# Sigmoid attention and a gated feed-forward layer on one core: another order of the step table

## The chip, the cores and the metric

The kernel runs on one core of one Trainium2 chip. The metric is the device time of one execution in microseconds. The engines are named as in the profile: PE (TensorE, matmuls), DVE (VectorE), ACT (ScalarE), POOL (GpSimd) and SP (SyncE). POOL and SP also issue the transfers: loads go through POOL's queue, stores through SP's.

## The reference

Two layers follow each other. The first is attention with a sigmoid in place of the softmax, over 8 batches, 12 heads, 448 tokens and a head size of 64. The second is a feed-forward layer of 768 to 2048 to 768 over all 3584 tokens, with a swish whose slope differs for each hidden column.

```python
scores = (1/sqrt(64)) * q @ k.T - log(448)      # for each batch and head
attn   = 1 / (1 + exp(-scores))
x      = (attn @ v)  -> 3584 x 768              # heads side by side
h      = x @ w_in                               # 768 -> 2048
g      = h * (1 / (1 + exp(-beta * h)))
out    = g @ w_out                              # 2048 -> 768, float32
```

## The kernel before

All matmuls are in float16. The heads of a batch are taken four at a time, as a group of two slots of two heads; there are 24 groups, three for each batch. The feed-forward layer takes the first batches with plain products and the rest with Strassen-like products: seven products, P1 to P7, in place of eight, at the price of sums of operands on DVE.

After an opening that is written out, the whole work is a table of 762 steps, `STEPS` (line 650). `follow` (line 638) runs it from left to right. A step issues its instructions to the engines' queues, and every engine works its queue off in that order, waiting on semaphores. So the table is the order on every engine. A step is a letter and its numbers:

- `Vg.j` is a visit: the scores of group g against the j-th block of keys. PE writes two score tiles (line 218) and ACT turns each into sigmoids, `attnT` (line 230). There are two score tiles in PSUM, so a visit can't begin before ACT has read the ones of the visit before.
- `Ag` multiplies the sigmoids of group g by v (line 291); DVE casts the result to `xT` (line 300).
- `D` and `O` are the plain products of the two halves of the feed-forward layer, `dense1` and `dense2`. An `O` step is an eighth of a product.
- `Ib.d.p` is product P*p* of the first half of the layer for batch b and block d (`wino1`): six matmuls of 224 columns, then an eviction. P1 is copied by ACT (line 463), P2 goes through ACT's sigmoid (line 425), the others are added by DVE (line 372), and after P3 one more DVE product (line 477) is made.
- `Ut.p.part` is half of product P*p* of the second half of the layer for tokens t and t+1 (`wino2`): four matmuls of 384 columns. After the second part of P3 and of P4 the rows of t and t+1 are stored, four transfers each (line 602).
- `G` and `B` are the sigmoid on ACT and the product on POOL that finish a block (lines 492 and 502). `X`, `H`, `S` and `T` are sums of operands on DVE (line 372). `R` is the transposition of q or k on DVE.
- `Q` loads q and k of a group, two transfers (line 115). `K` loads v of a batch, six transfers (lines 136 and 143). `E` copies rows of v on DVE.

A block of `I` and a pair of `U` take two output buffers `osb` each out of four. So a block or pair uses the buffers of the one two places before it again, and its evictions wait until the stores from them have landed. While visits are left, all products share four PSUM banks; P7 and P4 of an `I` block use the same bank, as do P5 and P3, so P4's matmuls wait until DVE has read P7's result.

One more thing hangs on the order. For each step `follow` looks for the next visit or attention step behind it. If it is an attention step, the products of this step are made in two halves of 64 output columns, with twice as many matmuls and weight loads:

```python
tiled["cols"] = D if then == "A" else P
RUN[step[0]](*(int(x) for x in step[1:].split(".")))
```

Of the kernel before, what the change touches and what calls it, by code (L numbers as in the profile page):

```python
# [13 lines left out]
def kernel(  # L14
# [623 lines left out]
    def follow(steps):  # L638
# [35 lines left out]
        B3.2.1 I3.3.2 I3.3.7 I3.3.3 V14.3 I3.3.4 U10.1.0 B3.3.0 B3.3.1 H10.2 R16.0 U10.1.1 A14 V15.2
        U10.2.0 H10.0 U10.7.0 H10.1 G3.3 U10.2.1 U10.5.0 U10.6.0 U10.6.1 H10.3 U10.5.1 X4.0 V15.0
        U10.7.1 X4.1 U10.3.0 U10.3.1 I4.0.1 I4.0.6 I4.0.5 H12.0 U10.4.0 X4.2 U10.4.1 X4.3 I4.0.2
        I4.0.3 I4.0.7 V15.1 E5 K6 G4.0 Q19 H12.2 U12.1.0 H12.1 U12.1.1 A15 R17.0 V16.1 U12.2.0 R18.1
        I4.0.4 B4.0.0 U12.6.0 B4.0.1 U12.2.1 U12.5.0 V16.2 U12.6.1 U12.5.1 I4.1.1 H12.3 I4.1.6
        U12.7.0 U12.7.1 R17.1 I4.1.5 U12.3.0 U12.3.1 I4.1.2 V16.0 R18.0 I4.1.3 U12.4.0 I4.1.7
        U12.4.1 Q20 G4.1 V16.3 I4.1.4 A16 B4.1.0 B4.1.1 R19.0 V17.2 I4.2.1 I4.3.1 I4.2.6 I4.2.5  # L680
        V17.1 I4.2.2 Q21 I4.2.7 I4.2.3 G4.2 V17.0 I4.2.4 I4.3.6 B4.2.0 I4.3.5 I4.3.7 I4.3.2 B4.2.1
        R20.0 I4.3.3 G4.3 V18.2 I4.3.4 R19.1 A17 I5.0.1 B4.3.0 X5.0 B4.3.1 U14.1.0 V18.0 I5.0.2 X5.1
        I5.0.6 Q22 I5.0.5 U14.1.1 V18.1 X5.2 X5.3 H14.0 I5.0.3 U14.2.0 E6 H14.2 K7 I5.0.7 H14.1
        V18.3 G5.0 U14.2.1 A18 V19.2 I5.0.4 U14.6.0 U14.5.0 U14.7.0 B5.0.0 U14.6.1 U14.5.1 B5.0.1
        U14.7.1 I5.1.1 V19.0 H14.3 I5.1.6 I5.1.2 U14.3.0 R21.1 U14.3.1 R20.1 V19.1 U14.4.0 E7 I5.1.5
        I5.1.7 U14.4.1 I5.1.3 V20.0 R21.0 I5.1.4 G5.1 B5.1.0 I5.2.1 B5.1.1 A19 V20.2 I5.2.6 Q23
        I5.2.5 I5.2.2 I5.2.7 I5.2.3 I5.3.1 I5.2.4 G5.2 I5.3.6 B5.2.0 V20.3 I5.3.5 I5.3.7 B5.2.1
        I5.3.2 I5.3.3 I5.3.4 V20.1 X6.0 B5.3.1 H16.2 B5.3.0 U16.1.0 U16.1.1 A20 V21.2 U16.2.0 H16.0
        U16.7.0 U16.2.1 G5.3 V21.0 H16.1 U16.5.0 R23.1 U16.6.0 U16.6.1 H16.3 U16.5.1 U16.7.1 H18.2
        I6.0.1 X6.2 V21.1 U16.3.0 X6.1 U16.3.1 U16.4.0 U16.4.1 I6.0.6 R22.1 I6.0.2 R22.0 I6.0.5 A21  # L690
        V22.0 H18.0 X6.3 I6.0.3 H18.1 U18.1.0 U18.7.0 U18.1.1 V22.1 I6.0.7 U18.6.0 U18.6.1 V22.2
        I6.0.4 H18.3 U18.5.0 G6.0 U18.2.0 R23.0 U18.5.1 U18.2.1 B6.0.1 B6.0.0 U18.7.1 V22.3 U18.3.0
        U18.3.1 U18.4.0 U18.4.1 I6.1.1 I6.1.6 A22 V23.0 I6.1.5 I6.1.7 I6.1.2 I6.1.3 I6.2.1 G6.1
        I6.1.4 B6.1.0 I6.2.6 I6.2.5 B6.1.1 I6.2.2 V23.1 I6.2.7 I6.2.3 I6.3.1 I6.2.4 I6.3.6 G6.2
        B6.2.1 I6.3.5 B6.2.0 I6.3.7 I6.3.2 I6.3.3 V23.2 I6.3.4 B6.3.1 U20.1.0 H20.2 U20.1.1 A23
        U20.7.0 B6.3.0 U22.1.0 H20.0 U20.2.0 H20.1 X7.0 U20.2.1 U20.5.0 U20.6.0 G6.3 U20.6.1 I7.0.1
        U20.5.1 H20.3 X7.2 U22.1.1 U20.7.1 I7.0.2 X7.1 U20.3.0 U20.3.1 U22.2.0 U22.2.1 H22.0 U20.4.0
        X7.3 H22.2 H22.1 U20.4.1 U22.5.0 I7.0.6 I7.0.5 U22.7.0 I7.0.7 I7.0.3 U22.6.0 G7.0 I7.0.4
        I7.1.1 I7.1.6 I7.1.5 B7.0.0 B7.0.1 I7.1.2 I7.1.7 I7.2.1 I7.1.3 I7.2.6 G7.1 I7.1.4 I7.2.5
        I7.2.7 B7.1.0 B7.1.1 U22.6.1 I7.2.2 I7.2.3 U22.5.1 H22.3 I7.2.4 I7.3.1 I7.3.6 B7.2.0 I7.3.5  # L700
        G7.2 B7.2.1 I7.3.7 U22.7.1 I7.3.2 I7.3.3 U24.1.0 I7.3.4 U22.3.0 U22.3.1 U24.1.1 U22.4.0
        B7.3.0 U22.4.1 U24.2.0 B7.3.1 H24.0 U26.1.0 U24.2.1 H24.1 U24.5.0 G7.3 U24.6.0 H24.2 U24.6.1
        U24.5.1 H24.3 H26.0 U24.7.0 U24.7.1 U26.1.1 U24.3.0 U24.3.1 H26.1 U24.4.0 U26.2.1 U26.5.0
# [137 lines left out]
```

## Time and profile before

| | us |
|---|---|
| median of 3 runs | 368.29 (367.94 to 368.37) |
| the profiled execution, as timed | 368.51 |
| its span, first to last instruction | 366.7 |
| outside the span | 1.8 |
| PE busy | 361.6 (99%) |
| DVE busy | 271.7 (74%) |
| ACT busy | 248.7 (68%) |
| POOL busy | 154.3 (42%) |

The granted TensorE clock was 1.0 throughout. The first matmul of the table starts 34.26 us into the span and the last one at 363.22. Matmuls are pipelined and the profile models their ends, so a busy share of 99% says that PE always had a matmul in flight, and not that none of them was late. How late they were is read from the starts: from the start of a step's first matmul to the start of the next step's.

### The profile page before, as it was taken

The numbers are of one execution on the slowest core, as the hardware profiler recorded it, in microseconds if no ns is written. First come the engines' busy times: TensorE is split into PE (matmuls) and PEld (weight loads), VectorE is DVE, ScalarE is ACT, GpSimd is POOL, SyncE is SP. The second block draws the span as 40 slices with busy tenths as digits, with TensorE's granted clock in tenths as the row PEclk, the third lists the DMA queues.
The fourth block names the chain that finished last, engine by engine and source line by source line (L and its number), as shares of the span: only waits on it lengthen the run. The fifth ranks groups of instructions, "written<-read, shape, count | busy, mean of one in ns | idle before, by whom it ended". The sixth has DMA issues, their size and how long they took to land.

```text
span 366.7 us, 9126 instructions
## 1 busy us (share of the span) xinstructions
PE 361.6 (99%) x3677; PEld 238.0 (65%) x3677; DVE 271.7 (74%) x521; ACT 248.7 (68%) x409; POOL 154.3 (42%) x192
## 2 busy tenths in 40 slices
...
GB/s 168 184 197 201 199 206 198 236 39 2 50 139 52 160 152 2 74 64 111 156 13 149 52 137 52 49 81 89 52 1 89 2 88 2 0 88 0 56 68 138
...
## 3 DMA queue, kind: packets, MB, share of 16 engines
...
q14 instruction: 13, 0.11, 0.1%
...
## 4 chain that ended last, share of the span: by engine, by line
PE 93%; DMA 3%; ACT 2%; DVE 1%; SPq 0%; issue 0%; ACTq 0%; DVEq 0%
PE m_ps L171 71%; PE sco L218 12%; PE av_ps L291 9%; DMA out_dram<-osb 2%; ACT attnT L230 1%; PE idle_ps L740 1%; DMA gt<-in_k_dram 1%; DVE osb L372 0%; SPq L602 0%; ACT osb L425 0%; DVE xT L300 0%; DVE kT L204 0%; ACT raw L749 0%; ACT osb L463 0%; SPq L723 0%
## 5 line engine op out<-in xcount | busy, mean ns | idle before, releaser
L230 ACT ACTIVATE attnT<-sco 128x896 f16<-128x896 f32 (+1 forms) x163 | 139.2, 908 | 37.8 <-PE sco L218 37.1
L372 DVE TENSOR_TENSOR osb<-m_ps,osb 128x448 f32<-128x448 f32 (+2 forms) x197 | 116.3, 596 | 51.1 <-PE m_ps L171 42.0
L171 PEld LDWEIGHTS <-w_in 128*128 128x128 f16 (+1 forms) x948 | 81.0, 100 | 18.8 <-issue 11.0
L171 PE MATMUL m_ps<-xT,w_in 128*128 128x224 f16 (+3 forms) x750 | 85.5, 266 | 0.3 <-ACT attnT L230 0.2
L492 POOL TENSOR_TENSOR gt<-osb,sg 128x448 f16<-128x448 f32 x26 | 29.5, 1135 | 117.8 <-ACT sg L425 107.7
L502 POOL TENSOR_TENSOR gt<-osb,sg 128x448 f16<-128x448 f32 x52 | 58.3, 1138 | 35.1 <-ACT sg L425 33.5
L425 ACT ACTIVATE sg<-osb,beta_sb 128x224 f32<-128x224 f32 (+1 forms) x104 | 54.0, 575 | 10.3 <-DVE osb L372 10.0
L171 PEld LDWEIGHTS <-sum 128*128 128x128 f16 (+1 forms) x444 | 39.9, 99 | 27.4 <-issue 3.6
L171 PEld LDWEIGHTS <-gt 128*128 128x128 f16 (+1 forms) x474 | 36.9, 102 | 25.7 <-issue 7.5
L171 PE MATMUL m_ps<-w_out,gt 128*128 128x384 f16 (+2 forms) x350 | 52.6, 324 | 0.0
L218 PE MATMUL sco<-qT,kT 32*128 32x448 f16 (+3 forms) x864 | 51.5, 340 | 0.3 <-ACT attnT L230 0.2
L171 PEld LDWEIGHTS <-w_S 128*128 128x128 f16 (+1 forms) x486 | 43.9, 99 | 7.0 <-issue 6.0
L171 PE MATMUL m_ps<-w_out,sum 128*128 128x384 f16 (+1 forms) x228 | 40.6, 327 | 0.0
L171 PE MATMUL m_ps<-w_T,sum 128*128 128x384 f16 (+1 forms) x216 | 40.3, 326 | 0.0
L300 DVE CAST xT<-av_ps 128x448 f16<-128x448 f32 (+1 forms) x54 | 28.4, 566 | 14.2 <-PE av_ps L291 14.1
L291 PE MATMUL av_ps<-attnT,v 128*64 128x448 f16 (+3 forms) x400 | 38.2, 343 | 0.0
L171 PE MATMUL m_ps<-xs,w_S 128*128 128x224 f16 (+1 forms) x330 | 36.2, 259 | 0.0
L291 PEld LDWEIGHTS <-v 128*64 128x64 f16 (+1 forms) x432 | 20.4, 108 | 17.7 <-issue 9.8
L425 ACT ACTIVATE osb<-m_ps,beta_sb 128x224 f32<-128x224 f32 x52 | 20.4, 448 | 15.4 <-PE m_ps L171 15.1
L218 PEld LDWEIGHTS <-kT 32*128 32x128 f16 (+1 forms) x864 | 13.5, 96 | 23.1 <-issue 21.5
L320 DVE TENSOR_TENSOR gt<-m_ps,sg 128x224 f16<-128x224 f32 (+1 forms) x40 | 16.6, 434 | 12.5 <-ACT sg L317 12.2
L463 ACT COPY osb<-m_ps 128x448 f32<-128x448 f32 x26 | 13.8, 535 | 17.7 <-PE m_ps L171 15.5
...
## 6 DMA issues: line engine op xcount, KB each, us to landing
...
w_in<-in_moe_w_in_dram POOLq DMA_DIRECT2D x8, 384.0 KB, 10.3
w_out<-in_moe_w_out_dram POOLq DMA_DIRECT2D x4, 768.0 KB, 13.1
...
```

The costliest lines, as they stand in the source:

```text
L171: nc.tensor.matmul(to[c : c + step], hidden[:, c : c + step], weights, **({} if step == P else {"tile_position": (0, c)}), **flags,)
L218: nc.tensor.matmul(sco[base : base + nk, hh, u0 : u0 + n], kT[g][lo : lo + BLK, jt * P : jt * P + nk, e], qT[g][lo : lo + BLK, c0 : c0 + n ...
L230: nc.scalar.activation(out=at[:, :, 0:n], in_=sco[:, :, 0:n], func=AF.Sigmoid, bias=NEG_LOG_S, scale=MSCALE,)
L291: nc.tensor.matmul(av[hh * D : (hh + 1) * D, 0:n], vs[b][base : base + nk, 2 * (s % NPAIR) + hh, jt], at[base : base + nk, hh, 0:n], start ...
L300: nc.vector.tensor_copy(out=xTs[b][:, s % NPAIR, c0 : c0 + n], in_=av[:, 0:n])
L320: nc.vector.tensor_tensor(out=gt[:, dc, off : off + n], in0=m1[:, 0:n], in1=sg[:, 0:n], op=ALU.mult)
L372: nc.vector.tensor_tensor(out=out, in0=in0, in1=in1, op=op)
L425: nc.scalar.activation(out=out, in_=in_, func=AF.Sigmoid, bias=0.0, scale=beta_sb[:, dc : dc + 1])
L463: nc.scalar.copy(out=oa[:, 0], in_=m)
L492: nc.gpsimd.tensor_tensor(out=gt[:, 2 * d : 2 * d + 2, off : off + QH], in0=ob[:, 0], in1=sg, op=ALU.mult)
L502: nc.gpsimd.tensor_tensor(out=gt[:, dc, off : off + S].rearrange("p (h n) -> p h n", h=2), in0=oa[:, :, j], in1=sg, op=ALU.mult,)
L740: nc.tensor.matmul(idle[:, 0:cols], still[:, 0:P], still[:, 0:cols], start=True, stop=True)
```

## The change

The table holds the same 762 steps in another order, made by a search that tried orders against several jittered executions. Opening, PSUM banks, products, buffers and the functions behind the letters are the same. Only the number of steps made in 64-column halves moves with the order: 65 in place of 50, which makes 80 more matmuls. The diff replaces the whole table; these are the lines that the prediction speaks of:

```diff
...
-        D0.11 D0.15 O0.0.4 R5.0 V4.2 O0.0.5 S1.1 O0.0.6 O1.0.2 O1.0.3 S1.0 O0.0.7 S2.0 O1.0.4 V4.3
...
-        V6.1 D1.10 D1.9 E2 K3 D1.1 X1.1 V6.3 T1.0 D1.0 A6 V7.1 I1.3.6 I1.3.2 X1.2 I1.3.5 V7.0 X1.3
-        I1.3.7 I1.3.3 I1.2.1 I1.3.4 G1.3 I1.2.6 B1.3.0 V7.2 R8.1 I1.2.5 I1.2.7 R8.0 B1.3.1 I1.2.2
...
-        U4.2.1 R11.0 U4.3.1 U4.4.1 R11.1 I2.1.1 V10.2 Q13 Q14 I2.1.6 I2.1.5 I2.1.7 I2.1.2 K4 I2.1.3
-        V10.3 I2.1.4 G2.1 B2.1.0 R12.1 I2.2.1 B2.1.1 A10 V11.0 I2.2.6 I2.2.5 R12.0 I2.2.7 I2.2.2
...
-        U8.2.1 U8.5.1 U8.7.0 V13.2 U8.7.1 U8.3.0 I3.0.4 U8.4.0 R16.1 B3.0.0 B3.0.1 U8.3.1 V14.0
-        U8.4.1 I3.1.1 A13 V14.1 I3.1.6 K5 I3.1.5 I3.1.7 I3.1.2 I3.1.3 I3.2.1 I3.1.4 Q18 I3.2.6 G3.1
-        B3.1.0 B3.1.1 I3.2.2 I3.2.5 V14.2 I3.2.7 I3.2.3 Q17 I3.3.1 I3.2.4 G3.2 I3.3.6 I3.3.5 B3.2.0
...
+        R5.1 O0.0.3 O1.0.0 O0.0.4 O0.0.5 V4.2 O1.0.1 S2.0 O1.0.2 O1.0.3 O0.0.6 O1.0.4 V4.3 S4.1 Q7
...
+        V6.1 T2.1 T4.1 D1.1 D1.10 R7.0 V6.0 D1.8 D1.11 E2 V6.3 X1.2 I1.3.5 Q10 I1.3.2 A6 K3 V7.0
+        I1.3.3 I1.3.7 G1.3 I1.2.1 V7.1 I1.3.4 I1.2.6 I1.2.5 R8.0 B1.3.0 U2.1.0 B1.3.1 R8.1 V7.2
...
+        U4.5.0 I2.0.7 Q13 R11.0 U4.2.0 U4.5.1 V10.1 U4.7.0 R11.1 U4.7.1 I2.0.4 U4.2.1 H4.3 B2.0.0
+        U4.4.0 V10.3 G2.0 B2.0.1 R12.1 U4.3.0 U4.3.1 A10 V11.1 I2.1.1 U4.4.1 I2.1.6 I2.1.5 I2.1.2
+        V11.0 I2.1.7 K4 I2.1.3 I2.2.1 I2.1.4 G2.1 B2.1.0 I2.2.6 B2.1.1 I2.2.5 I2.2.2 I2.2.7 V11.2
...
+        R14.1 H8.1 U8.1.0 U8.5.0 U8.1.1 V13.0 U8.6.0 U8.6.1 U8.5.1 U8.7.0 H8.3 U8.2.0 V13.2 R14.0 K5
+        I3.0.7 U8.2.1 G3.0 U8.7.1 U8.3.0 U8.3.1 R15.0 V14.1 I3.0.4 B3.0.0 U8.4.0 B3.0.1 U8.4.1
+        I3.1.1 A13 V14.0 I3.1.6 I3.1.5 I3.1.2 I3.1.7 I3.1.3 Q16 Q17 I3.2.1 I3.1.4 G3.1 B3.1.0 I3.2.6
+        I3.2.5 B3.1.1 I3.2.2 V14.2 I3.2.7 I3.2.3 I3.3.1 I3.2.4 I3.3.6 G3.2 B3.2.1 I3.3.5 R16.0
...
```

More of the change, by code (lines that the diff above doesn't have):

```diff
@@ L650 @@
     STEPS = """
-        R3.1 R3.0 D0.6 D0.12 R4.1 D0.14 D0.7 V3.1 R4.0 D0.13 D0.0 D0.8 V3.0 D0.3 D0.9 V3.3 D0.1
-        D0.10 E1 D0.2 Q6 V3.2 D0.4 O0.0.0 D0.5 O0.0.1 O0.0.2 V4.1 O1.0.0 O0.0.3 A3 V4.0 O1.0.1 R5.1
-        D0.11 D0.15 O0.0.4 R5.0 V4.2 O0.0.5 S1.1 O0.0.6 O1.0.2 O1.0.3 S1.0 O0.0.7 S2.0 O1.0.4 V4.3
-        O1.0.5 A4 V5.1 O1.0.6 O0.1.0 O0.1.1 O1.1.0 S2.1 Q7 T3.1 O1.0.7 S4.0 T2.1 O0.1.2 V5.0 T3.0
-        O0.1.3 O1.1.1 K2 O1.1.2 O1.1.3 O0.1.4 O0.1.5 V5.2 T2.0 O1.1.4 O0.1.6 O0.1.7 R6.1 O1.1.5 R6.0
@@ L656 @@
-        A5 O1.1.6 I1.3.1 V6.2 O1.1.7 S4.1 D1.8 R7.0 S3.1 D1.11 T1.1 Q8 V6.0 Q9 D1.3 R7.1 D1.2 X1.0
-        V6.1 D1.10 D1.9 E2 K3 D1.1 X1.1 V6.3 T1.0 D1.0 A6 V7.1 I1.3.6 I1.3.2 X1.2 I1.3.5 V7.0 X1.3
-        I1.3.7 I1.3.3 I1.2.1 I1.3.4 G1.3 I1.2.6 B1.3.0 V7.2 R8.1 I1.2.5 I1.2.7 R8.0 B1.3.1 I1.2.2
-        I1.2.3 I1.2.4 V8.0 U2.1.0 H2.2 B1.2.1 B1.2.0 R9.1 U2.1.1 R9.0 A7 V8.1 H2.0 H2.1 T4.1 T4.0
-        U2.7.0 U2.2.0 U2.2.1 Q10 V8.2 U2.5.0 U2.6.0 U2.6.1 X2.0 S3.0 H2.3 E3 V8.3 U2.5.1 A8 G1.2
-        X2.1 V9.1 U2.7.1 U2.3.0 U2.3.1 H4.0 I2.0.1 R10.0 V9.2 H4.2 I2.0.6 U2.4.0 I2.0.5 U2.4.1
@@ L662 @@
-        I2.0.2 H4.1 I2.0.3 R10.1 X2.2 U4.1.0 V9.0 X2.3 U4.1.1 Q11 G2.0 U4.6.0 U4.6.1 Q12 A9 V10.0
-        I2.0.7 H4.3 U4.5.0 U4.7.0 U4.5.1 V10.1 U4.7.1 I2.0.4 B2.0.1 U4.3.0 U4.4.0 U4.2.0 B2.0.0
-        U4.2.1 R11.0 U4.3.1 U4.4.1 R11.1 I2.1.1 V10.2 Q13 Q14 I2.1.6 I2.1.5 I2.1.7 I2.1.2 K4 I2.1.3
-        V10.3 I2.1.4 G2.1 B2.1.0 R12.1 I2.2.1 B2.1.1 A10 V11.0 I2.2.6 I2.2.5 R12.0 I2.2.7 I2.2.2
-        I2.2.3 I2.3.1 Q15 G2.2 V11.1 I2.3.6 I2.2.4 B2.2.1 B2.2.0 I2.3.5 I2.3.2 R13.1 I2.3.7 I2.3.3
-        V11.2 I2.3.4 B2.3.1 U6.1.0 B2.3.0 H6.2 U6.1.1 A11 H6.0 V12.2 U6.2.0 U6.7.0 H6.1 U6.2.1 G2.3
@@ L668 @@
-        V12.0 X3.0 U6.5.0 U6.6.0 U6.6.1 X3.1 U6.5.1 H6.3 I3.0.1 U6.7.1 I3.0.6 X3.2 V12.1 H8.0 E4
-        R13.0 U6.3.0 U6.3.1 U6.4.0 U6.4.1 I3.0.5 R15.0 Q16 V12.3 H8.2 I3.0.2 A12 H8.1 V13.1 I3.0.3
-        R14.0 U8.1.0 U8.1.1 U8.5.0 U8.6.0 G3.0 I3.0.7 U8.6.1 V13.0 X3.3 R15.1 H8.3 U8.2.0 R14.1
-        U8.2.1 U8.5.1 U8.7.0 V13.2 U8.7.1 U8.3.0 I3.0.4 U8.4.0 R16.1 B3.0.0 B3.0.1 U8.3.1 V14.0
-        U8.4.1 I3.1.1 A13 V14.1 I3.1.6 K5 I3.1.5 I3.1.7 I3.1.2 I3.1.3 I3.2.1 I3.1.4 Q18 I3.2.6 G3.1
-        B3.1.0 B3.1.1 I3.2.2 I3.2.5 V14.2 I3.2.7 I3.2.3 Q17 I3.3.1 I3.2.4 G3.2 I3.3.6 I3.3.5 B3.2.0
@@ L674 @@
[L674 to L703, printed above, removed]
@@ L704 @@
-        U26.6.0 H26.2 U26.6.1 U26.5.1 H26.3 U26.7.0 U26.7.1 U24.4.1 U26.3.0 U26.3.1 U26.4.0 U26.4.1
+        R3.1 R3.0 D0.7 D0.0 D0.12 D0.10 V3.0 D0.2 D0.4 R4.0 R4.1 D0.6 D0.11 V3.1 D0.13 D0.14 E1 V3.3
+        D0.3 D0.5 D0.8 V3.2 S1.1 S1.0 D0.9 Q6 D0.1 O0.0.0 O0.0.1 S2.1 V4.1 O0.0.2 A3 V4.0 D0.15 R5.0
+        R5.1 O0.0.3 O1.0.0 O0.0.4 O0.0.5 V4.2 O1.0.1 S2.0 O1.0.2 O1.0.3 O0.0.6 O1.0.4 V4.3 S4.1 Q7
+        O0.0.7 A4 V5.2 O0.1.0 O0.1.1 O0.1.2 O0.1.3 O1.1.0 O1.0.5 V5.0 T3.0 O1.0.6 O0.1.4 K2 O0.1.5
@@ new lines @@
+        T2.0 O1.1.1 O1.1.2 T3.1 O0.1.6 X1.0 V5.1 O0.1.7 S3.1 T1.0 O1.0.7 O1.1.3 O1.1.4 A5 O1.1.5
+        O1.1.6 X1.1 R6.1 R6.0 I1.3.1 O1.1.7 X1.3 D1.9 D1.3 T1.1 V6.2 D1.0 R7.1 Q8 Q9 D1.2 I1.3.6
+        V6.1 T2.1 T4.1 D1.1 D1.10 R7.0 V6.0 D1.8 D1.11 E2 V6.3 X1.2 I1.3.5 Q10 I1.3.2 A6 K3 V7.0
+        I1.3.3 I1.3.7 G1.3 I1.2.1 V7.1 I1.3.4 I1.2.6 I1.2.5 R8.0 B1.3.0 U2.1.0 B1.3.1 R8.1 V7.2
+        I1.2.7 I1.2.2 I1.2.3 V8.0 I1.2.4 H2.2 B1.2.1 U2.1.1 A7 B1.2.0 V8.1 U2.7.0 R9.0 U2.2.0 U2.2.1
+        H2.0 H2.1 V8.2 R9.1 X2.0 T4.0 U2.5.0 U2.6.0 U2.6.1 H2.3 V8.3 R10.0 U2.5.1 G1.2 U2.7.1 A8
@@ new lines @@
+        V9.0 H4.0 U2.3.0 X2.2 U2.3.1 X2.1 I2.0.1 U2.4.0 S4.0 S3.0 U2.4.1 V9.2 I2.0.6 Q11 I2.0.2
+        I2.0.5 U4.1.0 H4.1 X2.3 V9.1 E3 R10.1 I2.0.3 U4.6.0 U4.1.1 V10.2 Q12 H4.2 U4.6.1 A9 V10.0
+        U4.5.0 I2.0.7 Q13 R11.0 U4.2.0 U4.5.1 V10.1 U4.7.0 R11.1 U4.7.1 I2.0.4 U4.2.1 H4.3 B2.0.0
+        U4.4.0 V10.3 G2.0 B2.0.1 R12.1 U4.3.0 U4.3.1 A10 V11.1 I2.1.1 U4.4.1 I2.1.6 I2.1.5 I2.1.2
+        V11.0 I2.1.7 K4 I2.1.3 I2.2.1 I2.1.4 G2.1 B2.1.0 I2.2.6 B2.1.1 I2.2.5 I2.2.2 I2.2.7 V11.2
+        I2.2.3 I2.3.1 I2.2.4 I2.3.6 I2.3.5 B2.2.1 G2.2 B2.2.0 R12.0 I2.3.7 I2.3.2 I2.3.3 U6.1.0
@@ new lines @@
+        I2.3.4 G2.3 B2.3.0 U6.1.1 R13.1 A11 B2.3.1 H6.0 V12.0 H6.1 I3.0.1 X3.0 U6.2.0 U6.2.1 V12.2
+        H6.2 U6.5.0 Q15 U6.6.0 X3.1 U6.6.1 I3.0.2 R13.0 X3.3 V12.1 I3.0.6 H6.3 I3.0.5 Q14 U6.5.1
+        X3.2 U6.7.0 H8.0 U6.7.1 U6.3.0 V12.3 U6.3.1 E4 I3.0.3 U6.4.0 R15.1 H8.2 U6.4.1 A12 V13.1
+        R14.1 H8.1 U8.1.0 U8.5.0 U8.1.1 V13.0 U8.6.0 U8.6.1 U8.5.1 U8.7.0 H8.3 U8.2.0 V13.2 R14.0 K5
+        I3.0.7 U8.2.1 G3.0 U8.7.1 U8.3.0 U8.3.1 R15.0 V14.1 I3.0.4 B3.0.0 U8.4.0 B3.0.1 U8.4.1
+        I3.1.1 A13 V14.0 I3.1.6 I3.1.5 I3.1.2 I3.1.7 I3.1.3 Q16 Q17 I3.2.1 I3.1.4 G3.1 B3.1.0 I3.2.6
@@ new lines @@
+        I3.2.5 B3.1.1 I3.2.2 V14.2 I3.2.7 I3.2.3 I3.3.1 I3.2.4 I3.3.6 G3.2 B3.2.1 I3.3.5 R16.0
+        I3.3.2 I3.3.7 B3.2.0 I3.3.3 V14.3 I3.3.4 B3.3.0 B3.3.1 H10.2 U10.1.0 U10.1.1 A14 V15.0 H10.0
+        U10.7.0 H10.1 G3.3 U10.2.0 U10.2.1 U10.5.0 R17.0 U10.6.0 U10.6.1 H10.3 X4.0 U10.5.1 U10.7.1
+        I4.0.1 H12.0 V15.1 U10.3.0 E5 U10.4.0 X4.1 Q18 U10.3.1 X4.2 I4.0.6 U10.4.1 R16.1 I4.0.5
+        I4.0.2 I4.0.7 X4.3 K6 H12.1 V15.2 U12.1.0 I4.0.3 I4.0.4 U12.1.1 U12.6.0 R17.1 R18.0 B4.0.0
+        U12.5.0 V16.0 U12.6.1 B4.0.1 H12.2 U12.2.0 U12.5.1 U12.2.1 G4.0 A15 V16.2 Q19 I4.1.1 I4.1.6
@@ new lines @@
+        U12.7.0 U12.7.1 V16.1 I4.1.2 H12.3 I4.1.5 U12.3.0 U12.3.1 I4.1.3 V16.3 I4.1.7 R18.1 U12.4.0
+        U12.4.1 I4.1.4 G4.1 B4.1.0 A16 B4.1.1 V17.2 I4.2.1 I4.2.6 I4.2.5 V17.0 I4.3.1 Q20 I4.2.2
+        I4.2.7 I4.2.3 V17.1 I4.2.4 I4.3.6 B4.2.0 I4.3.5 B4.2.1 I4.3.2 I4.3.7 I4.3.3 G4.2 Q23 V18.2
+        I4.3.4 B4.3.1 R19.0 X5.0 E6 A17 B4.3.0 I5.0.1 U14.1.0 G4.3 X5.1 V18.1 R19.1 U14.1.1 I5.0.2
+        I5.0.6 I5.0.5 V18.0 U14.2.0 H14.0 X5.2 U14.2.1 I5.0.3 V18.3 I5.0.7 X5.3 H14.1 A18 V19.0
+        H14.2 Q21 I5.0.4 U14.6.0 U14.6.1 R21.0 V19.1 K7 B5.0.1 R20.0 H14.3 U14.7.0 U14.5.0 U14.5.1
@@ new lines @@
+        U14.7.1 G5.0 B5.0.0 V19.2 R20.1 I5.1.1 U14.3.0 U14.3.1 U14.4.0 I5.1.6 I5.1.5 U14.4.1 I5.1.2
+        I5.1.7 I5.1.3 R21.1 V20.0 E7 G5.1 I5.1.4 B5.1.0 I5.2.1 A19 B5.1.1 V20.2 I5.2.6 I5.2.5 I5.2.7
+        I5.2.2 I5.2.3 I5.2.4 Q22 G5.2 I5.3.1 B5.2.0 I5.3.6 V20.3 U16.1.0 I5.3.5 B5.2.1 I5.3.7 R23.0
+        I5.3.2 I5.3.3 V20.1 I5.3.4 H16.2 B5.3.0 R23.1 U16.1.1 B5.3.1 A20 H16.0 V21.2 U16.7.0 H16.1
+        U16.2.0 U16.2.1 V21.0 R22.1 U16.5.0 U16.6.0 U16.6.1 H16.3 U16.5.1 U16.7.1 X6.0 V21.1 X6.1
@@ new lines @@
+        R22.0 G5.3 U16.3.0 U16.3.1 A21 V22.1 H18.0 I6.0.1 X6.2 H18.1 I6.0.6 U16.4.0 U16.4.1 V22.0
+        H18.2 I6.0.5 U18.1.0 I6.0.2 U18.6.0 I6.0.3 U18.1.1 U18.6.1 V22.3 I6.0.7 U18.5.0 U18.5.1
+        U18.7.0 H18.3 X6.3 V22.2 U18.2.0 I6.0.4 U18.7.1 U18.2.1 G6.0 B6.0.0 B6.0.1 U18.3.0 U18.4.0
+        U18.3.1 U18.4.1 I6.1.1 A22 V23.0 I6.1.6 I6.1.5 I6.1.2 I6.1.7 I6.1.3 I6.2.1 I6.1.4 G6.1
+        I6.2.6 B6.1.1 B6.1.0 I6.2.5 I6.2.2 V23.1 I6.2.7 I6.2.3 I6.3.1 I6.2.4 I6.3.6 I6.3.5 G6.2
+        B6.2.1 B6.2.0 I6.3.2 I6.3.7 I6.3.3 V23.2 I6.3.4 B6.3.0 H20.2 U20.1.0 U20.1.1 B6.3.1 A23
```

9 lines of the change are left out of this document (added).

## The prediction

> **What bounds the kernel now.** I read the page first, then PE's own waits, then PE's rows in order of time, and last the chain of waits around the one place where PE was held.
>
> The page, its first rows:
>
> ```profile
> span 366.7 us, 9126 instructions
> ...
> PE 361.6 (99%) x3677; PEld 238.0 (65%) x3677; DVE 271.7 (74%) x521; ACT 248.7 (68%) x409; POOL 154.3 (42%) x192
> ```
>
> What PE waited for (us in total, times, longest):
>
> ```profile
> PE idle_ps L740 <- DVE gt L733: 1.2, 1, 1.2
> PE m_ps L171 <- ACT attnT L230: 0.2, 1, 0.2
> PE sco L218 <- ACT attnT L230: 0.2, 1, 0.2
> ```
>
> PE has nearly no visible wait, and the other engines have a quarter of the span to spare. But an idle row appears only once the pipeline has run dry, so I took PE's pace from the starts of its steps. PE's timeline near 106 us (start, length, what):
>
> ```profile
> 105.69 0.74 PE L171 MATMUL m_ps<-xT,w_in 128*128 128x224 f16 x6
> 106.27 0.74 PE L171 MATMUL m_ps<-xT,w_S 128*128 128x224 f16 x6
> 106.84 0.81 PE L171 MATMUL m_ps<-w_out,gt 128*128 128x384 f16 x4
> 107.59 0.57 PE L218 MATMUL sco<-qT,kT 32*128 32x448 f16 x8
> 108.09 0.84 PE L171 MATMUL m_ps<-w_out,gt 128*64 128x384 f16 x8
> ```
>
> An `I` step takes 106.84 - 106.27 = 0.57 us, a `U` step ahead of a visit 0.75, the visit 0.50. I laid the whole table on these rows, step by step. Each kind of step, with the kind that follows it, has one pace: `I` 0.577, `U` 0.651, `O` 0.328, visit 0.507, attention 1.548; a `U` or `I` ahead of a visit takes 0.095 more. All paces together make 327.7 us from the table's first matmul (34.26) to its last step. Starts later than that pace add up to 0.66 us: four visits 0.04 late each, and two starts late by 0.24 and 0.25, at 179.82 and 181.21. So all waiting that another order could remove is 0.66 us, 0.18% of the time.
>
> The chain of waits that leads to 181.21 (start, us, what):
>
> ```profile
> 171.03 5.74 DMA out_dram<-osb
> ...
> 176.95 0.79 ACT osb L425 x2
> ...
> 178.42 0.93 ACT attnT L230
> 179.34 0.43 ACT osb L463
> ...
> 180.53 0.64 DVE osb L372
> ...
> 181.21 0.73 PE m_ps L171 x6
> ```
>
> The last store of pair U8, issued at 171.03, took 5.74 us, beside the loads of K5 (issued from 168.33). P2 of block I3.2 needs that buffer. Its matmuls began at 175.02, and a result is ready 0.75 after the start, at 175.77; ACT began at 176.95, 1.18 late. Behind it ACT's queue held the visit's sigmoids and P1's copy of I3.3, and PE lost 0.49. So that place had 0.69 of slack.
>
> **The change part by part.** *PE's amount.* Steps, functions and order of modes are alike: I counted 173 changes between full, 64-column, visit and attention matmuls in both tables. What differs is the 65 steps in halves in place of 50. The rows price them: an `I` in halves 0.590 against 0.577, ten more of them, 0.13; a `U` 0.660 against 0.651, seven more, 0.06; one `O` and one `D1` fewer in halves, -0.03. In all +0.16 us, on the path.
>
> One rule of the Trainium skill speaks against these steps. "TensorEngine Tiling (Array Packing)", section Restrictions, says that column tiling switches the fast weight load off, and "TensorE: Matmul & The Clock Gate", section LDWEIGHTS, gives a load as its columns divided by 1.2, in ns: 53 for 64 columns, an estimated 0.64 us for an `I` in halves. By that the ten steps would cost 0.6 and the sum below would be half a us higher. The trace's 16 such steps take 0.58 to 0.60, so the row decides.
>
> *The store wait goes.* In the old table K5 is behind B3.0.0 and B3.0.1, so POOL issues its six loads among U8's stores. In the new one K5 is ahead of G3.0 and B3.0.0; the POOL work ahead of it is B2.3, and its v buffer is free after A11, so the loads leave at about 144 to 147. U8's stores, at 165.5 to 169.2 by the paces, have no load beside them (Q16 and Q17 come behind them); 45 of the 105 stores of the trace, those with nothing beside them, land in 1.7 to 1.9. That is -0.49. Next late there is P2 of I3.2, whose result comes some 5 us after the last landing.
>
> *Visits too close.* There are two score tiles, so a visit waits for ACT on the one before. At 220.96 a visit starts, ACT reads its tiles from 221.57 for 1.73 us, and the next visit, at 223.29, has its second tile 0.04 late. So 2.38 us between visits is the least without a wait. The old table has four that come 0.04 late, 2.34 to 2.41 apart (0.17 in all). The new one has three at 2.34 (0.13; two more, at 2.38 and 2.41, could add 0.08) and V4.2 to V4.3: one visit 0.507, four `O` of 0.328 and one of 0.421 make 2.24, so 0.14 late. The old V4.2 to V4.3 held five `O` more than the last, 2.57.
>
> *One bank.* I1.3.4 adds onto the bank that I1.3.7 opened, and must wait for DVE's add of it. The new table puts I1.3.3 first. With t the end of I1.3.3 on PE: DVE starts its add at t+0.20, then the line 477 product at t+0.74, then I1.3.7's add at t+1.27, done and seen by PE at t+1.95. PE is there after I1.3.7 (0.58), I1.2.1 (0.67) and V7.1 (0.51), at t+1.76, of which 0.03 is V7.1's own wait. Late by 0.16.
>
> *What stays hidden.* The other moves (`R`, `S`, `T`, `X`, `H` on DVE; `G`, `B` on POOL; `Q` with two loads, `K` with six) keep each engine's amount, and DVE is idle for 95 us, POOL for 212. The nearest to the path is the second column half of w_out: its last part lands at 57.67 (issued in the unchanged opening), and O0.1.4, its first reader, moves from 60.4 to 59.2, so 2.7 us of cover becomes 1.5. If that landing came 2 us later the cost would be 0.5. I take 0.
>
> *Sum.* 0.16 - 0.49 - 0.17 + 0.13 + 0.14 + 0.16 = -0.07 us. The profiled execution took 368.51 (its span and 1.8), so 368.44 by it. It lay 0.22 above the median of the runs; on the median it is 368.2.
>
> **The rivals.** *The store wait comes back at another pair (slower).* In the new table K4 is right behind U4.4.1, so its six loads (issued at about 124.5 to 127.5) meet the four stores of U4's second tile (125.1 to 126.2). P2 of I2.2 needs that buffer; its result is ready at about 130.9. With 0.19 from landing to ACT and the 0.69 of slack seen before, PE loses time once the last store takes over 130.9 - 0.19 + 0.69 - 126.2 = 5.2 us. For it: the like meeting in the old table took 5.74, which would cost 0.5 (368.7). Against it: with six loads and no `Q` beside them, stores after K6 took 2.9 to 3.5. It decides over 0.74 us from 6.0 us of landing; the longest store of the trace, beside ten loads, took 6.14, which gives 0.9 and 369.1. By the longest late v load, 8.97, it would be 3.8 and 372.
>
> *Many thin places (slower).* In the old table 17 of PE's 543 waits in the table were released less than 0.11 us before PE came. The new order has two real misses already, counted above. DVE's adds of one form differ by 0.04 us from row to row. If 20 to 30 places miss by that, it is 0.8 to 1.2 us, 369.0 to 369.4. Against it: in the trace of before hardly any of them missed.
>
> *All waits gone (faster).* If the new places don't miss and nothing replaces the old ones: -0.66 + 0.16 = -0.50, 367.8. That is still within 0.2% of before; PE's pace is the floor, and the opening is the same. To go beyond needs something that these rows don't show.
>
> *The change does nothing for speed:* a search against jitter may buy steadiness alone. It would look like my forecast.
>
> **How the numbers follow.** A difference of 0.2% (0.74 us) is about what a measurement of this kernel can tell from none. My forecast, -0.5 to +0.7, has 0.70; the store wait over its point 0.13; the thin places 0.11; faster by more 0.06. The time is 368.2. The range goes down to 367.6, the floor of 367.8 less the runs' own spread, and up to 369.4, the end of the thin places; the far end of the store wait and part of the faster case are left out, about 0.1.
>
> **What would show it.** In the new profile: no start late near 180, and ACT's line 425 there straight behind PE; V4.3's second tile late by about 0.1 near 53 us; I1.3.4 late by 0.16 near 83.6; U4's second stores, near 125, landing in under 5.2 us; `I` steps in halves at 0.59. I am wrong if late starts add up to over 1.2 us, or if the paces themselves differ.

## The result and the profile after

The changed kernel takes 370.61 us (median of 6 runs, 369.97 to 371.33), the kernel before 368.32 beside it (6 runs, 367.94 to 368.74). The ratio is 1.0062, with a 95% interval of 1.0049 to 1.0076: slower by 2.3 us, above the forecast's range.

The page of the changed kernel, its first rows:

```profile
span 369.6 us, 9291 instructions
...
PE 362.5 (98%) x3757; PEld 238.8 (65%) x3757; DVE 273.3 (74%) x521; ACT 248.3 (67%) x409; POOL 153.8 (42%) x192
```

There are 80 more matmuls, as counted, and 0.9 us more of busy PE. What PE waited for (us in total, times, longest):

```profile
PE m_ps L171 <- DVE xs L372: 1.3, 1, 1.3
PE idle_ps L740 <- DVE gt L733: 1.2, 1, 1.2
PE m_ps L171 <- DVE osb L372: 0.6, 1, 0.6
```

The middle row belongs to the opening and stood there before. The first and the last are new. Laid on the paces of the prediction, PE's late starts add up to 3.02 us, where they were 0.66: 0.14 at V4.3, 0.19 at I1.3.4, 1.07 in three steps at 134 to 138 us, 1.43 at 233.8 us, 0.19 in three small ones. From the table's first matmul to its last it is 331.38 us against 328.96, so 2.42 more, and 2.36 of it are late starts. The first matmul itself starts 0.39 later than before (34.65 us); over the twelve profiles of the two orders and their variants it starts at 33.86 to 34.65, so no run shows that part to be the order's. Two places hold 2.50 of the 3.02.

The first of the two: U4's stores, and ACT at P2 of I2.2, which needs their buffer. In the changed kernel, the tile view of the output from 120 to 134 us, then ACT's timeline (start, length, what, idle time before it):

```profile
L602 SPq DMA_DIRECT2D out_dram<-osb x8: 314/422/430, 122.4 to 127.0; - x8
...
DMA to landing us min/median/max: 1.8/2.4/6.2
```

```profile
129.56 2.03 ACT L425 ACTIVATE sg<-osb,beta_sb 128x224 f32<-128x224 f32 x4
133.34 0.78 ACT L425 ACTIVATE osb<-m_ps,beta_sb 128x224 f32<-128x224 f32 x2 [1.74 <-PE m_ps L171]
```

The last store left at 126.95 and landed 6.2 us later, at 133.16; K4's loads were issued from 125.13 to 128.8. PE had the product ready at about 131.4 (its matmuls began at 130.66), so ACT's 1.74 us of idle time is not PE's, although the row names PE: ACT began 0.18 after the landing.

The second place: DVE's `X5.1` and POOL, from the timelines of the two engines in the changed kernel, and PE behind them:

```profile
230.94 0.59 POOL L115 DMA_DIRECT2D raw<-in_q_dram  x1
231.53 0.53 POOL L115 DMA_DIRECT2D raw<-in_k_dram  x1
232.07 2.24 POOL L502 TENSOR_TENSOR gt<-osb,sg 128x448 f16<-128x448 f32 x2
234.28 1.12 POOL L492 TENSOR_TENSOR gt<-osb,sg 128x448 f16<-128x448 f32 x1
...
231.97 1.16 DVE L300 CAST xT<-av_ps 128x448 f16<-128x448 f32 x2
233.16 2.61 DVE L372 TENSOR_TENSOR xs<-xT,xs 128x672 f16<-128x672 f16 x1
...
233.82 0.74 PE L171 MATMUL m_ps<-xT,w_in 128*128 128x224 f16 x6
235.83 1.32 PE L171 MATMUL m_ps<-xs,w_S 128*128 128x224 f16 x12 [1.27 <-DVE xs L372]
```

`X5.1`, a sum of two SBUF tiles (the row of 672 columns), takes 2.61 us; the other 27 of its form take 0.50 (median). It ends at 235.77, which is 0.37 behind the last of POOL's three products (235.40). I5.0.6 on PE needs it. In the kernel before, DVE's and POOL's timelines have the same sum begin in a pause of POOL, and the loads come behind the products:

```profile
231.76 0.51 DVE L372 TENSOR_TENSOR xs<-xT,xs 128x672 f16<-128x672 f16 x1
...
232.07 2.29 POOL L502 TENSOR_TENSOR gt<-osb,sg 128x448 f16<-128x448 f32 x2 [1.37 <-PE sco L218]
234.31 0.60 POOL L115 DMA_DIRECT2D raw<-in_q_dram  x1
```

### The profile page after: what moved, and what is told of

Read it like the earlier page. It is cut to its first block, busy times and chain, and to the rows that moved or that the text cites. A ratio compares the mean times of both kernels' runs of the same rounds, so it can differ in the third digit from the quotient of the medians.

```text
span 369.6 us, 9291 instructions
## 1 busy us (share of the span) xinstructions
PE 362.5 (98%) x3757; PEld 238.8 (65%) x3757; DVE 273.3 (74%) x521; ACT 248.3 (67%) x409; POOL 153.8 (42%) x192
## 4 chain that ended last, share of the span: by engine, by line
PE 94%; DVE 2%; ACT 1%; DMA 1%; issue 1%; SPq 0%; DVEq 0%
PE m_ps L171 72%; PE sco L218 12%; PE av_ps L291 9%; ACT attnT L230 1%; PE idle_ps L740 1%; DMA gt<-in_k_dram 1%; DVE xs L372 1%; DVE osb L372 1%; DVE xT L300 0%; DVE qT L196 0%; DVE kT L204 0%; ACT raw L749 0%; SPq L723 0%; DVE v L146 0%; DVE gt L477 0%
## 5 line engine op out<-in xcount | busy, mean ns | idle before, releaser
L171 PE MATMUL m_ps<-xT,w_in 128*128 128x224 f16 (+2 forms) x762 | 85.0, 265 | 0.2 <-ACT attnT L230 0.2
L115 POOL DMA_DIRECT2D raw<-in_q_dram x26 | 15.0, 577 | 27.8 <-DVE qT L196 13.9
L136 POOL DMA_DIRECT2D v<-in_v_dram x32 | 19.9, 636 | 13.1 <-DMA w_out<-in_moe_w_out_dram 6.6
```

Of the source, the lines that this page charges most:

```text
L115: nc.gpsimd.dma_start(out=raws[g][:, r, c0:c1].rearrange("p c d -> p (c d)"), in_=(q, k)[r][b, HQ * t : HQ * (t + 1)].rearrange("h (p c) d ...
L136: nc.gpsimd.dma_start(out=vs[b][i * BLK : (i + 1) * BLK, :, 0:JF].rearrange("p h j d -> p h (j d)"), in_=rows[:, :, JF * i * D : JF * (i + ...
L171: nc.tensor.matmul(to[c : c + step], hidden[:, c : c + step], weights, **({} if step == P else {"tile_position": (0, c)}), **flags,)
```

## The experiments

Theory A: the loss is these two meetings, K4's loads with U4's stores and POOL's products with `X5.1`. The rivals: many thin places, a loss that moves on wherever the order sends it, or a difference that is luck of one profile. Later the question became what makes `X5.1` so long. Ratios are to the kernel before, timed on the same chip.

**The new table once more (again), K4 sooner (k4_early), POOL's products later (x51_apart), both (both_moves).**

```diff
# k4_early
-  U4.5.0 I2.0.7 Q13 R11.0 ...      V11.0 I2.1.7 K4 I2.1.3
+  U4.5.0 I2.0.7 Q13 K4 R11.0 ...   V11.0 I2.1.7 I2.1.3
# x51_apart
-  E6 A17 B4.3.0 I5.0.1 U14.1.0 G4.3 X5.1 V18.1 R19.1
+  E6 A17 I5.0.1 U14.1.0 X5.1 V18.1 B4.3.0 G4.3 R19.1
```

> The new table once more, unchanged, to see which of its late starts come back. Theory A (two collisions: K4's loads delay the store that P2 of I2.2 waits for, 1.07 us in the profile; X5.1 on DVE stood still beside three products of POOL, 1.43 us): 370.6 us again, and both places late again in this profile. Rival B (the loss is spread: the opening 0.4, the halves, many thin places that differ from run to run): 370.6 too, but late starts at other places, and neither of the two over 0.5 us.

> K4 right behind Q13, so that its six loads are over before U4's stores. Theory A: the last store of U4's second tile lands in 1.9 instead of 6.2 us, no start late between 133 and 138 us, 1.0 us less than the new table: 369.6. Rival B: the same time as the new table within 0.3.

> B4.3.0 and G4.3 behind V18.1, so that their products on POOL come after X5.1 on DVE. Theory A: X5.1 takes 0.5 us instead of 2.6, I5.0.6 isn't late, 1.4 us less than the new table where that collision happens in every run: 369.2. If it happens in some runs only, 0.7 less. Rival B: the same time as the new table within 0.3, with another operation late in its place.

> Both moves. Theory A: the two add up, 2.4 us less than the new table, 368.2, level with the kernel before. Rival B: 370 or more.

| | us | ratio | late starts | at 134 to 138 | at `X5.1` |
|---|---|---|---|---|---|
| again | 370.24 | 1.0046 [1.0029, 1.0063] | 2.80 | 0.85 | 1.43 |
| k4_early | 369.94 | 1.0035 [1.0022, 1.0048] | 2.06 | 0 | 1.43 |
| x51_apart | 369.78 | 1.0034 [1.0019, 1.0048] | 2.07 | 0.45 | 0, then 1.11 |
| both_moves | 369.47 | 1.0027 [1.0014, 1.0039] | 1.61 | 0 | 0, then 1.10 |

The places are the table's and no luck: `again` shows the same ones. The three moves gained less than expected (369.6, 369.2 and 368.2 us). With K4 sooner the stores land within 1.9 us and ACT is straight behind PE, but the median falls by 0.3 us only, where the profile of `again` lost 0.85: the loss at this place differs from run to run, as the landings below show. k4_early in the two views of above:

```profile
DMA to landing us min/median/max: 1.8/1.9/1.9
...
131.39 0.78 ACT L425 ACTIVATE osb<-m_ps,beta_sb 128x224 f32<-128x224 f32 x2
```

`x51_apart` takes the meeting away, `X5.1` is back at 0.51 us. But most of it is lost again 4 us later, in DVE's timeline:

```profile
232.20 0.51 DVE L372 TENSOR_TENSOR xs<-xT,xs 128x672 f16<-128x672 f16 x1
...
236.93 0.69 DVE L372 TENSOR_TENSOR sum<-gt 128x1024 f16<-128x1024 f16 x1 [1.29 <-POOL gt L492]
```

H14.0 waits for the product that I had put later, DVE's queue stands behind it, and PE is late by 0.31 and 0.80. A move that clears one meeting made the next wait.

**The same with the products in another place and Q23 one product later (x51_apart_2, both_moves_2), and the kernel before once more (before_again).**

```diff
# x51_apart_2; both_moves_2 has K4 behind Q13 besides
-  G4.2 Q23 V18.2 I4.3.4 B4.3.1 R19.0 X5.0 E6 A17 B4.3.0 I5.0.1 U14.1.0 G4.3 X5.1 V18.1
+  G4.2 V18.2 I4.3.4 B4.3.1 Q23 R19.0 X5.0 E6 A17 I5.0.1 U14.1.0 X5.1 G4.3 B4.3.0 V18.1
```

> After's table with POOL's last products of batch 4 moved away from X5.1 in both directions: B4.3.0 goes behind X5.1, G4.3 straight behind X5.1 and ahead of B4.3.0, and Q23 behind B4.3.1. In x51_apart the later G4.3 made H14.0 wait on DVE for 1.29 us and cost PE 0.31 and 0.80. Theory A (what costs is the collision of X5.1 with the products, and H14.0's wait for G4.3 when G4.3 comes too late): X5.1 takes about 0.5 us, H14.0 waits for less than 0.4 us, PE has no late start over 0.2 us between 230 and 245 us; what is left is the store wait near 134 to 137 us (0.45 to 1.07 us) and about 0.5 us of small ones: 368.7 to 369.2 us. Rival (the loss is bound to the amount of DVE and POOL work in this stretch, and goes wherever the order sends it): a late start of 0.8 us or more shows up again between 230 and 245 us, and the time stays at 369.8 us.

> The edit of x51_apart_2 and K4 behind Q13, as in k4_early. Theory A: both collisions are gone and neither is given back: late starts of 0.4 to 0.6 us in all (0.14 at V4.3, 0.19 at I1.3.4, the rest small), so 368.2 to 368.6 us, level with the kernel before (0.998 to 1.001 of it). Rival 1 (many thin places, or slower paces, are the rest of the loss): the two places are clean and the time is still 369.2 us or more. Rival 2 (the loss moves on): a late start of 0.8 us or more elsewhere, 369.4 us.

> The kernel before, unchanged, profiled a second time beside the others. Theory A: its late starts add up to 0.5 to 0.9 us again, of which about 0.5 from U8's last store; no DVE operation with two SBUF inputs takes over 1 us. Rival (its 0.66 us was a lucky profile, and the difference lies in luck): over 1.5 us of late starts in this one.

`x51_apart_2` took 368.98 us, 1.0009 [0.9995, 1.0023]: `X5.1` 0.51 us, no late start over 0.04 between 230 and 245, 0.53 left at the stores, 1.04 in all. `both_moves_2` took 368.22, 0.9993 [0.9984, 1.0001]: late starts of 0.65 in all, as many as before. The kernel before beside them had 368.45 (23 runs). So with both meetings gone the 2.3 us are gone, little is left for thin places (0.19 us), and the new order is level with the old one; no version here is shown to be faster. What PE waited for in both_moves_2 no longer has a row of `xs` or `osb`:

```profile
PE idle_ps L740 <- DVE gt L733: 1.2, 1, 1.2
PE m_ps L171 <- ACT attnT L230: 0.2, 1, 0.2
PE sco L218 <- DVE kT L204: 0.2, 1, 0.2
PE sco L218 <- ACT attnT L230: 0.2, 1, 0.2
```

The second profile of before has 0.88 of late starts: 0.24 behind U8's stores (longest landing 5.4 us), 0.51 at the first `O` step, where PE waited for the first part of w_out, and the rest small. It has no sum of 672 columns over 0.51 us.

**What does a sum wait for? (lock_alone)** This kernel, like the other `lock_` ones, leaves the computation out and stores zeros. It only starts DVE operations and POOL products side by side:

```python
for op in (sums, long_sums, evict, turn, copy16):
    for n in (0, 1, 2, 3, 0, 1, 2, 3):
        nc.vector.memset(a32[:, 0:8], 0.0)           # releases POOL
        products(n, a32)                             # n products of 128x448 f32
        nc.vector.tensor_copy(out=c32, in_=pt[:, 0:S])
        op()
        ...
```

> This kernel leaves the whole computation out and stores zeros; it only starts DVE operations beside POOL's products. Five kinds of DVE operation (a sum of 128x672 f16 from two SBUF tiles as X5.1 is; the same over 1024 columns; a sum of one PSUM and one SBUF tile; a 32x32 transpose; a copy from one SBUF tile) start beside 0, 1, 2 and 3 products of 128x448 f32 in a row on POOL (1.12 us each in the traces). Theory A (DVE's operation with two SBUF inputs and POOL's products share one way into SBUF, and the one that came first keeps the other out, product after product): the sums take about 0.50 us with 0 products, and beside n products they end only after the last of them, so about 1, 2 and 3 us, growing by about 1.1 us for each product; the PSUM sum keeps its time within 0.1 us; the copy and the transpose, with one input, are not known from the traces of the table and may go either way. Rival B (both engines merely share SBUF's bandwidth): the sums get longer by a share of their length, at most doubled (1.0 us), the long ones by more than the short ones, and no further growth from 1 to 3 products. Rival C (X5.1's 2.61 us is time that it waited for its input, not the product's): the sums take 0.50 us whatever POOL does.

DVE's and POOL's timelines, the sum beside three products:

```profile
10.52 3.56 POOL L61 TENSOR_TENSOR p<-a,b 128x448 f16<-128x448 f32 x3 [0.37 <-DVE a L69]
10.81 1.20 DVE L45 TENSOR_TENSOR z<-x,y 128x672 f16<-128x672 f16 x1
```

The sum takes 0.50 us alone and 1.14 to 1.20 beside one, two or three products: it ends 0.36 behind the first product (10.52 + 1.13 = 11.65; 10.81 + 1.20 = 12.01), and the second product waits for it (three take 3.56 us in place of 3.30). The long sum goes from 0.68 to 1.38, the f16 copy from one SBUF tile from 0.32 to 1.02. The sum with one input in PSUM stays at 0.62, the transpose at 0.63. So there is an exclusive way: while one of the two uses it, the other stands still. Theory A's "product after product" is wrong here. B, a mere sharing of bandwidth, falls because the sum gets longer by more than its own length and the long sum by the same 0.70; C falls because the sum does get longer. 2.61 us was not explained.

The Trainium skill, "SBUF — State Buffer", section "Who interferes with whom", says that a DVE instruction with two SBUF inputs contends with a GpSimd instruction that reads SBUF, and that whoever issues first has the shared ports for the whole instruction while the other fully blocks. This run agrees (1.14 to 1.20 us beside a product, and a product that waits for the sum). By that rule `X5.1` would have waited for one product at the most: to 234.31 at the latest, ended by 234.68 and made PE at most 0.3 late, not 1.43.

**Does it depend on the moment? (lock_when, lock_when_fine, x51_sooner, x51_later)** The first two start the sum at many moments after the first of three products; the others shift `X5.1` in the table.

```diff
# x51_sooner
-  X5.0 E6 A17 B4.3.0 I5.0.1 U14.1.0 G4.3 X5.1 V18.1
+  X5.0 A17 B4.3.0 I5.0.1 U14.1.0 G4.3 X5.1 E6 V18.1
# x51_later
-  U14.1.0 G4.3 X5.1 V18.1 R19.1 U14.1.1
+  U14.1.0 G4.3 R19.1 X5.1 V18.1 U14.1.1
```

> Again the whole computation is left out and zeros are stored. lock_alone showed a sum that came 0.3 us after the start of the first of three products: it took 1.20 us, so it got in between the first product and the second. X5.1 in the new table came 0.07 us before the end of a product and got in only behind two more. Here the sum (128x672 f16, two SBUF tiles) is started at 31 grades of time after the first of three products began, from 0.3 to about 1.4 us, finest around that product's end, once with plain products and once with products in two halves and the sum in place, as the table's are. Theory A1 (the products pass the way on to each other unless the sum has been waiting for some time): sums that come up to about 1.0 us after the product's start end 0.37 us after that product; those that come in the last 0.1 to 0.2 us of it, or just behind the next one's start, end 0.37 us after the third product and take 2.4 to 2.7 us. Theory A2 (a sum always waits for just the product that is running): no sum takes over 1.4 us, and one that comes just behind the second product's start ends with the second; then the 2.61 us of X5.1 has another cause besides the products. Theory A3 (it depends on the products' or the sum's form): the two halves of the run differ at the same grade.

> lock_when's sums came 0.29 to 0.90 us or 1.18 to 1.89 us after the first product began, and each waited for just the product that ran then; none came between 0.90 and 1.18. X5.1 in the new table came at 1.09 (233.16 less 232.07), in the gap. This kernel (the computation is left out, zeros are stored) fills the gap in steps of about 0.01 us. Theory A1 (a sum that comes while one product hands over to the next misses both, and ends 0.37 us behind the third): somewhere between 0.90 and 1.18 the sum takes 2.5 to 2.7 us and ends at about 3.70 us from the first product's start, in a stretch of 0.02 to 0.2 us. Theory A2: every sum ends 0.37 us behind the product that was running (at 1.49 or at 2.58), none takes over 1.5 us, and X5.1's 2.61 us stays unexplained by products alone.

> After's table with E6 (a copy of 0.35 us on DVE ahead of A17's casts) moved behind X5.1, and nothing else: X5.1 comes about 0.3 us sooner, in the middle of the first of the three products. Theory A1 (what decides is when it comes): X5.1 waits for that one product, takes 0.7 to 0.9 us, PE is not late at I5.0.6, and the time is 1.4 us under the new table's, 368.6 to 369.2 us. Theory A3 (three products in a row keep DVE out whenever it comes): X5.1 takes 2.8 to 3.0 us, PE is late by 1.4 us and the time stays at 370.0 to 370.6 us.

> After's table with R19.1 (two transposes, 0.56 and 0.20 us on DVE) moved ahead of X5.1, and nothing else: X5.1 comes about 0.7 us later, at about 233.9, in the middle of the second product. Theory A1: it waits for that product alone, takes about 0.8 us, ends near 234.7, a whole us sooner than in the new table although it was put behind more work, and PE is late by 0.2 to 0.5 us at I5.0.6; 369.0 to 369.6 us. Theory A3 (the products keep DVE out to the last): X5.1 ends at 235.8 again and takes 1.9 us, PE late by 1.4 us, 370.0 to 370.6 us.

Measured alone, every sum waits for the running product only. Sums that come up to 0.98 us after the first product began end at 1.49 to 1.50; those that come at 0.99 to 1.09, as one product hands over to the next, take 0.50 and get in at once; from 1.12 on they take up to 1.46 and end at 2.58. Both forms of product give the same. In the table it is otherwise: x51_sooner's sum came 0.6 us after the first product began (231.00 after 230.41) and took 3.11 us, x51_later's came 1.6 after (232.00) and took 2.11, and both ended 0.37 behind the third product (234.11 after 233.74). PE lost 1.42 in each; 369.88 us, 1.0042 [1.0026, 1.0058], and 370.19, 1.0051 [1.0032, 1.0071]. The moment is not it. Something in the table differed from the bare products.

**What differs? (lock_forms)**

```python
if loads:                       # two loads on POOL's queue, as Q23
    load(0); load(1)
if by_act:                      # ACT writes the products' second inputs
    for i in range(3): nc.scalar.copy(out=sg[i]..., in_=pt[:, 0:S])
products(table_products)        # three, in the table's strides or plain
fill(...)
sums(table_sum)                 # as X5.1, or plain
```

> The computation is left out, zeros are stored. x51_sooner and x51_later showed that X5.1, at whatever moment it came, ended 0.37 us behind the last of the three products, while in lock_when_fine a sum never waited for more than the product that was running. This kernel puts the differences between the two in one at a time, in all 16 combinations, each at two moments: two loads issued on POOL ahead of the products (Q23 in the table) or none; the products' second inputs written by ACT just ahead (the sigmoids) or not; the products in the table's forms (inputs and outputs in strides) or plain; the sum in X5.1's form (three pieces of 224, one input in strides) or plain. Theory S (the sum's form: in strides its reading can't take the way between two products): all combinations with X5.1's form end about 0.37 us behind the third product, those with the plain sum behind the running one. Theory G (the products' form): the same split by the products. Theory L (the loads): the split goes by the loads; DVE is kept out while POOL still has loads and products in a row. Theory N (none of these): no sum waits for more than one product, and the cause stays open.

DVE's and POOL's timelines, products and sum in the table's forms, without loads and with them:

```profile
40.17 2.48 POOL L65 TENSOR_TENSOR gt<-oa,sg 128x448 f16<-128x448 f32 x2 [0.52 <-DVE ob L88]
40.62 1.04 DVE L52 TENSOR_TENSOR xs<-xT,xs 128x672 f16<-128x672 f16 x1
...
124.21 0.54 POOL L69 DMA_DIRECT2D raw<-in_k_dram  x1
124.75 2.23 POOL L65 TENSOR_TENSOR gt<-oa,sg 128x448 f16<-128x448 f32 x2
125.39 3.04 DVE L52 TENSOR_TENSOR xs<-xT,xs 128x672 f16<-128x672 f16 x1
126.93 1.13 POOL L66 TENSOR_TENSOR gt<-ob,sg 128x448 f16<-128x448 f32 x1
```

Without loads, all 16 cases end behind the product that was running; with loads and no work of ACT, all 8 end 0.37 behind the third (126.93 + 1.13 = 128.06; 125.39 + 3.04 = 128.43), whatever the forms. In the 8 cases with both, the sum came only with the third product or behind it, so they say nothing. Theory L stands, S and G fall.

**How do the loads do it, and is it so in the table? (lock_loads, q23_behind)** lock_loads varies loads, their queue, a pause and the number of products; q23_behind moves Q23 alone:

```diff
# q23_behind
-  G4.2 Q23 V18.2 ...   U14.1.0 G4.3 X5.1 V18.1
+  G4.2 V18.2 ...       U14.1.0 G4.3 Q23 X5.1 V18.1
```

> The computation is left out, zeros are stored. lock_forms split cleanly by one thing: with two loads issued on POOL just ahead of the three products, the sum ended 0.37 us behind the third product in every combination (3.0 to 3.2 us for one that came 0.5 us after the first began); without them behind the running one. Here the loads are varied: ahead of 1 to 6 products; one load in place of two; two loads issued by SP's queue; a pause on POOL of about 0.4 to 9 us between the loads and three products; one or two products ahead of the loads. Theory L1 (POOL's row of loads and products goes without a break, and DVE is kept out until POOL has a pause): the sum ends behind the last product for all of 1 to 6 products, a pause of any length ends the effect, loads of SP have none. Theory L2 (loads under way keep DVE out between products): the effect lasts as long as the loads run, 3 to 5 us from their issue, so with 6 products the sum gets in before the last, pauses under about 3 us leave the effect, longer ones end it; SP's loads may have it too.

> After's table with Q23 (the two loads that POOL issues ahead of B4.3.1, B4.3.0 and G4.3) moved behind G4.3, and nothing else: POOL's products then run in a row from about 230.9 on, four of them, with no load ahead, and X5.1 still comes among them. Theory L (the loads ahead make the lock-out): X5.1 waits for one product at most, takes under 1.6 us and mostly ends by 234.6, PE is late by under 0.4 us at I5.0.6, 369.0 to 369.5 us. Theory A3 (products in a row are enough): X5.1 ends 0.37 us behind the last product again; as the products end about 1.1 us sooner, at 234.3, PE is late by 0.3 us. The two are told apart by X5.1's own time and end in the trace, not by the total.

lock_loads, the timelines of POOL and DVE: two loads and six products; then the sum with no load and four products; the sum with SP's load; two loads and a pause:

```profile
41.97 0.54 POOL L63 DMA_DIRECT2D raw<-in_k_dram  x1
42.51 6.55 POOL L56 TENSOR_TENSOR m<-a,b 128x448 f16<-128x448 f32 x6
43.01 6.43 DVE L53 TENSOR_TENSOR xs<-xT,xs 128x672 f16<-128x672 f16 x1
...
50.53 1.35 DVE L53 TENSOR_TENSOR xs<-xT,xs 128x672 f16<-128x672 f16 x1
...
68.49 1.35 DVE L53 TENSOR_TENSOR xs<-xT,xs 128x672 f16<-128x672 f16 x1
...
76.33 0.54 POOL L63 DMA_DIRECT2D raw<-in_k_dram  x1
77.63 3.56 POOL L56 TENSOR_TENSOR m<-a,b 128x448 f16<-128x448 f32 x3 [0.76 <-DVE a L92]
77.88 1.24 DVE L53 TENSOR_TENSOR xs<-xT,xs 128x672 f16<-128x672 f16 x1
```

Behind two loads the sum takes 1.30, 2.11, 3.18, 4.27, 5.34 and 6.43 us for one to six products, always to 0.37 behind the last. One load in place of two does the same (2.66 us for a sum that came 1.02 after the first of three). Products ahead of the loads change nothing: the sum still waits to the last product behind them. A load of SP has no effect; only the first of the two was issued by then, and it writes float32, where POOL's loads convert to float16. A pause of 0.76 us on POOL, which waits for DVE there, ends the effect, and all longer ones do; yet the loads were still under way then (they landed 7.3 and 8.9 us after their issue). So L1 holds: what counts is that a load stands ahead of the products in POOL's unbroken row (instructions without idle time between them), and not the transfer. Nor do the loads alone hold DVE up: in x51_apart_2 `X5.1` came at 232.28, while POOL issued Q23's two loads (232.00 to 233.13), and took 0.51 us. Why the engine does so, no run shows; pauses under 0.76 us were not tried.

`q23_behind` took 369.00 us, 1.0008 [0.9996, 1.0021]. Its timelines of POOL, DVE and PE:

```profile
230.27 2.24 POOL L502 TENSOR_TENSOR gt<-osb,sg 128x448 f16<-128x448 f32 x2 [0.80 <-ACT sg L425]
232.47 1.41 POOL L492 TENSOR_TENSOR gt<-osb,sg 128x448 f16<-128x448 f32 x1
233.83 0.59 POOL L115 DMA_DIRECT2D raw<-in_q_dram  x1
...
231.65 1.23 DVE L372 TENSOR_TENSOR xs<-xT,xs 128x672 f16<-128x672 f16 x1
...
232.93 1.32 PE L171 MATMUL m_ps<-xs,w_S 128*128 128x224 f16 x12
```

`X5.1` still comes amid three products. It waits for the second (to 232.51), takes 1.23 us, and the third waits for it (1.41 in place of 1.12). PE is late by 0.05. By PE's late starts, two loads moved behind three products are worth 1.4 us.

## Why the prediction was wrong

**The step that failed is "What stays hidden".** It cleared the moved `X`, `G`, `B` and `Q` because each engine kept its amount, with DVE idle for 95 us and POOL for 212. Amounts don't say who meets whom: in the old order `X5.1` came in a pause of POOL of 1.37 us, ahead of its products, and the loads came behind them; in the new one Q23 is ahead of three products in a row and `X5.1` falls among them. That is 1.43 us that no term of the sum and no rival had. Without it the time is within the range: q23_behind took 369.00 us. A sign of the shared way was in the trace of before, small: a sum for `H` that took 0.8 us in place of 0.68 near 183.75 us, beside a product. That a load ahead makes it last for the whole row was not in that trace.

**The first rival came true, and its weight was the mistake.** It was given 0.13, and PE lost time there in five profiles of seven. The landing times of U4's last store and PE's loss, over the seven profiles with K4 at the new place:

| longest landing, us | 6.2 | 6.0 | 5.6 | 5.5 | 5.5 | 4.9 | 4.5 |
|---|---|---|---|---|---|---|---|
| PE late at 134 to 138, us | 1.07 | 0.85 | 0.53 | 0.45 | 0.38 | 0 | 0 |

The point of 5.2 us and the price beyond it (6.2 - 5.2 = 1.0 against 1.07) were right within 0.15 us. The stores behind K6, at 2.9 to 3.5 us, were the wrong rows to weigh by: the like meeting, at 5.74, was the one to go by. These landings differ from run to run, and so does the time of the new order.

**The rest held.** U8's stores landed in 1.8 to 1.9 us and nothing is late near 180 (-0.49, as said). V4.3's second tile is late by 0.137 (0.14 was said) and I1.3.4 by 0.19 (0.16). The paces are the same; what the halves cost is at most the 0.06 us that the late starts leave of 2.42, where the sum had 0.16. The thin places didn't open: 0.19 in three. The prediction named the sign itself: wrong if late starts exceed 1.2 us, and they are 3.02.
